# A state-space layer and a gated FFT convolution in one kernel: another order of its 815 operations

## The chip, the cores and the metric

The kernel runs on one core of one Trainium2 chip. The metric is the device time of one execution in microseconds. Three timed runs of the kernel before gave 187.6, 186.19 and 186.77 us; the median, 186.77, is the time that the change is held against.

## The reference

Two sequence layers on inputs of 2048 steps by 640 channels, written side by side into one output of 1280 channels:

```python
# A: a diagonal complex state-space layer
Lam_bar = exp(exp(log_dt) * (Lambda_re + 1j * Lambda_im))
B_bar = ((Lam_bar - 1) / Lambda)[:, None] * (B_re + 1j * B_im)
Bu = einsum("bld,pd->blp", x, B_bar)
h[t] = Lam_bar * h[t - 1] + Bu[t]                  # t = 0 .. 2047
y_A = 2 * einsum("blp,dp->bld", h, C).real + x * Dskip
# B: a short convolution, a gate, a long convolution, a gate
k_shift[t] = sum(k[t - 3 + i] * shift_k[:, 3 - i] for i in range(4)) # four taps
kv = k_shift * v
y = irfft(rfft(kv, 4096) * rfft(ssm_k, 4096))[:2048]
y_B = q * (y + kv * ssm_D)
out = concatenate([y_A, y_B], axis=-1)
```

All inputs and the output are bfloat16.

## The kernel before, in words

The program is built in two steps. First `build` calls methods of `PartA` and `PartB`, which record 815 operations with `Program.add`: a name, the engines that may do it, what it reads and writes in one large SBUF array (`arena`), and its PSUM group. Nothing is issued by that. Then `Program.emit` goes through the table `ORDER` (L1117) from left to right and issues each operation on the engine that stands in the table. An entry such as `561A4` is operation 561, on ScalarE (A; V is VectorE, G GpSimd, T TensorE, S the DMA queue of SyncE), with its PSUM group from bank 4 on. A small `t` is TensorE too, and puts the operation in `P.narrow`: its matmuls are then issued as two halves of 64 columns of weights each (`wide`, L225 for a whole one, L229 for a half; s1 has the same at L876 and L881). There are 8 banks, and most groups take two, so up to four groups are in flight. Each engine does its entries in the order of the table; waits between engines follow from what the operations read and write and from who held the bank last. So the table sets the order on each engine, the engine of each operation that has a choice, the banks, and the halves. Nothing else of the kernel decides an order.

Part A, the state-space layer, scans by a tree. The complex state is kept as pairs of real rows, ten groups of 128.

- up2, up1, up0: projections of x (`base`, L581) and additions of shifted terms by tables of powers (RR, made at L457 on VectorE; its matmuls are L602). ScalarE or VectorE copies the result out of PSUM (ev_up, L598, L622, L648).
- the coarse scan, in two halves 0 and 1: a swap by matmul (cs_v, cs_k, by `wide`), its product with a sine (cs_v_m, cs_k_m, L679), cs_a L682, cs_w L683, the scan cs_s L684, cs_b L687 and cs_h L690, all on VectorE.
- dn and ad: the way down, a matmul and an addition (L728 on VectorE; on ScalarE the sum is made by TensorE and L726 copies it).
- gC and ev_gC: C scaled by matmul (L571) and copied (L575).
- C0 to C15: 128 rows of the output each. ld_r loads rows of x (L736), xd multiplies them by Dskip (L737, on VectorE or GpSimd; Dskip is loaded by ld_Dr, L372), 20 matmuls make C (L225, or 40 halves at L229), and ev_C adds (L754 on VectorE; or a copy on ScalarE, L752, and the addition em_C on GpSimd, L760). L765 stores.

Part B, the gated convolution.

- per 128 channels: k and v come transposed (L814), the taps cm (L205 on VectorE, L206 on ScalarE), additions ca L840, the gate cx L841, and a copy to DRAM (pl, L847). The relay rl loads that back in another layout, eight pieces for each half of the channels (L857, sixteen in all).
- s1 and s2: the two stages of the forward transform, of the filter ("h", loaded at L807, with addD L809) and of kv ("k"), for each half (s1k0, s1k1 and so on), by matmuls (L876 or L881, then L900), with copies e1 (L886) and e2 (L913).
- the product of the two spectra, four pieces for each half: pp L924, pq L927, py L929, pz L931.
- r2 and r1: the two stages of the inverse transform (L951, L972). r2 of one half reads all four py and pz of that half. er2 copies (L956). er1 multiplies by q: on VectorE directly (L990), on ScalarE as a copy (L988) with the product em1 after it on VectorE or GpSimd (L995). q is loaded at L825, and L1006 stores.

The names carry the half and the first index: er10_22 is the eviction of r1 of half 0, block 22; cm3_2 is tap 2 of channel group 3. The table interleaves both parts on every engine.

Of the kernel before, what the change touches and what calls it, by code (L numbers as in the profile page):

```python
# [1097 lines left out]
def plain_order(P):  # L1098
# [19 lines left out]
    "168A0 156G0 161S0 0V0 58G0 6T0 17G0 167A0 162S0 110G0 19V0 147G0 87V0 11G0 18V0 89A0 90S0 12G0 3T1 42G0 13V0 88S0 182S0 "  # L1118
    "67G0 22V0 4T0 25V0 171T1 26G0 23V0 65V0 148G0 39V0 66V0 112G0 59V0 72G0 9T0 183S0 165T2 46G0 30G0 169T0 69G0 180S0 92T3 "
    "5T4 93V3 20V0 10T5 111G0 94A0 68G0 166A2 95V0 1T4 163T5 32V0 160G0 2T4 181S0 124V0 122V0 102V0 164A5 31V0 127V0 96V0 8T2 "  # L1120
    "103V0 21V0 104V0 61V0 172A1 7T4 126V0 105V0 28V0 14V0 106V0 219T2 60V0 101A0 107V0 100A0 36V0 98A0 108V0 170A0 123V0 37V0 "
    "173S0 38V0 128V0 33V0 109V0 40V0 62V0 114G0 317V0 113G0 125V0 27V0 115G0 29V0 41V0 116G0 117G0 149G0 221T0 220A2 174S0 "
    "118G0 43G0 97A0 99A0 119A0 44G0 211T2 222V0 155S0 63A0 151G0 378S0 71A0 15A0 47G0 70A0 209T0 212V2 152G0 45A0 120V0 50G0 "
    "121V0 178S0 213T2 131V0 210A0 52G0 143V0 159A0 74G0 187S0 179S0 217T0 381A0 146V0 51G0 34A0 227T4 380A0 129V0 186S0 48G0 "
    "130V0 185S0 214A2 382V0 77G0 215T6 218A0 54G0 132V0 228V4 157S0 73G0 383A0 237T0 133V0 35V0 82G0 134V0 184S0 216A6 83G0 "
    "384V0 49A0 379S0 55G0 261T6 385A0 56G0 78G0 253T4 53A0 386V0 79G0 75A0 389S0 262V6 238A0 225T2 150G0 254A4 188V0 176S0 "
    "57A0 84G0 387V0 201T4 154A0 177S0 195T6 245T0 196A6 202V4 390S0 226A2 391V0 392V0 191T2 246A0 136V0 229T4 393V0 269S0 "
    "192A2 394V0 76A0 395V0 153A0 223T2 396V0 230A4 144V0 400S0 141A0 203T0 224A2 189T4 135V0 145V0 239T6 81A0 388S0 64V0 397V0 "
    "204A0 401S0 140A0 190A4 398V0 199T0 193t2 16A0 138A0 231T4 403V0 194A2 137V0 24V0 402V0 271S0 142A0 200A0 404V0 80A0 197T0 "
    "405V0 240A6 247T2 406V0 198A0 232A4 399S0 407V0 86A0 408V0 444S0 241T6 248A2 205T0 242A6 315V0 249T2 139A0 206A0 233T4 "  # L1130
    "250A2 409V0 243T6 411S0 207T0 234A4 244A6 251T2 235T4 255T6 252A2 175V0 410S0 208A0 415S0 236A4 85A0 320V0 316V0 158S0 "
    "447V0 301T4 256A6 313T0 446V0 302A4 318t2 257T6 319V2 314A0 309T4 448V0 258A6 311T2 414S0 310A4 259T6 299T0 416S0 321V0 "
    "413S0 260A6 449V0 303T4 312A2 263T6 412S0 322V0 304A4 272S0 300A0 450V0 305T0 264A6 451V0 323t4 417S0 297T2 306A0 324V4 "
    "418S0 265T6 445S0 298A2 273T0 266V6 281T4 325V0 267T6 274A0 285T2 282V4 268A6 307T0 286A2 326V0 327t4 295T6 329V0 308A0 "
    "275T2 328V4 296A6 293T0 276V2 423t4 724S0 294A0 330V0 455S0 279T6 336T2 331V0 280A6 431T0 424A4 334V0 332T6 337A2 277T4 "
    "333V6 432A0 287T2 270S0 278V4 433T6 288A2 335V0 425T0 729S0 452V0 434A6 338t4 440S0 419T2 441S0 426A0 339V4 421T6 453G0 "
    "420A2 422V6 429t0 340t4 442S0 430A0 435T2 341V4 342t6 346t7 436A2 427T0 343V6 289T4 347V7 428A0 437t2 290V4 350t6 438A2 "
    "458V0 439S0 344t4 457V0 351A6 283T0 501T2 345V4 459G0 284A0 348t6 502A2 91S0 466T0 349V6 352t4 467A0 291T2 353V4 470T6 "
    "292A2 477T0 471A6 490T2 478V0 734S0 468T4 491A2 456S0 499T6 460V0 479T0 469A4 726t2 461V0 500A6 443V0 480A0 725V0 602S0 "
    "462A0 524t0 727V2 532t6 522t4 730V0 731T2 728S0 525A0 454S0 463V0 739S0 533A6 472V0 464G0 523A4 503T6 732V2 366t0 504A6 "  # L1140
    "481T4 744S0 367V0 528T2 482A4 358t6 529A2 514T4 359V6 368t0 515A4 520T2 369V0 356t6 521A2 518T4 735G0 465S0 357V6 519A4 "
    "354T0 733S0 492T2 603S0 355V0 493A2 516t4 740G0 488T6 517A4 526t2 474V0 530t0 527A2 741t4 475V0 531A0 483V0 749S0 489A6 "
    "608S0 605S0 594T6 485G0 604S0 742V4 590T0 595A6 588T2 591V0 584T4 589A2 607S0 582T6 745V0 598T0 736t2 606S0 599A0 486V0 "
    "473V0 585A4 609S0 494V0 583A6 600T4 596T6 737V2 601A4 496G0 372t0 597A6 586T4 373V0 592T2 587A4 580T6 593V2 374t0 581A6 "
    "612T4 497G0 375V0 610t2 613A4 618T6 611A2 619V6 616T4 628T0 617A4 624T2 484V0 620t6 625A2 505V0 746T4 621A6 476V0 629A0 "
# [83 lines left out]
```

## Time and profile before

| what | value |
|---|---|
| timed runs | 187.6, 186.19, 186.77 us |
| the profiled execution: span from the first to the last instruction | 187.3 us |
| the profiled execution's own time | not given beside the span |
| mean granted TensorE clock | 0.999 of full speed |
| DMA | 30.15 MB, mean 161 GB/s |
| instruction fetches on q8 | 26 packets, 0.43 MB |

How to read the lines that follow. The page gives for each engine its busy time in us, its share of the span, and the number of instructions (PE is TensorE's matmuls, PEld its weight loads, DVE VectorE, ACT ScalarE, POOL GpSimd). A line of the waits names the waiting engine and line, what it waited for, and then the total in us, the times, and the longest. A line of the timeline has the start, the duration, the engine and the line, the operation with output and input, the number of instructions, and in brackets the idle time before it and what ended it; `issue` stands where the profile shows nothing that was waited for. SPq is SyncE's queue of DMA issues: there the duration is that of issuing. In the line groups, the number behind the count is busy us, then mean ns of one, then idle us before them. A line of the windows has the stretch, its length, then busy us and instructions of PE, PEld, DVE, ACT and POOL, and the granted clock, the DMA share and GB/s.

### The profile page before, as it was taken

What the parts mean: (1) busy time and instruction counts of PE and PEld (TensorE: products, weight loads), DVE (VectorE), ACT (ScalarE), POOL (GpSimd) and SP (SyncE); (2) the same over time, 40 slices, a digit from 0 to 9 for tenths busy, and PEclk for the clock granted to TensorE, in tenths of its full rate; (3) what the DMA queues carried; (4) which work ended last, traced back from release to release, by engine and by line L of the source; (5) the groups of instructions that cost most, each with busy time, mean ns of one, the idle gap of its engine ahead of it and who ended that gap; (6) DMA issues with size and microseconds to landing.
All of it is one profiled execution on the core that took longest, in us unless ns stands there. A gap on an engine that the chain in (4) does not pass through costs nothing.

```text
span 187.3 us, 7665 instructions
## 1 busy us (share of the span) xinstructions
PE 175.6 (94%) x3398; PEld 126.3 (67%) x3399; DVE 158.0 (84%) x225; ACT 147.7 (79%) x181; POOL 72.6 (39%) x68
## 2 busy tenths in 40 slices
PE   7998999999799979979997999999999999999992
PEld 2565666677468756656685688776588876887770
DVE  3537964679959899999969999899999999998961
ACT  2469699989899979999997997997898883985000
POOL 8679999900000000008803925730740000551620
PEclk9999999999999999999999999999999999999999
DMA  5999999799999989999989479402496993058996
GB/s 153 191 184 158 200 143 140 141 174 182 198 253 154 290 179 152 180 182 154 138 109 251 154 170 133 75 5 72 122 196 120 210 227 85 15 160 187 208 219 173
DMA packets 106682, 30.15 MB, mean 161 GB/s; under 512 B 101274, under 2 KB 106010, under 8 KB 106650
## 3 DMA queue, kind: packets, MB, share of 16 engines
q1 hardware_dynamic: 106332, 29.35, 86.7%
q8 instruction: 26, 0.43, 1.1%
q10 hardware_dynamic: 318, 0.33, 0.6%
q14 instruction: 6, 0.05, 0.1%
HBM read 11.32 MB, written 7.86 MB: 102 GB/s over the span
## 4 chain that ended last, share of the span: by engine, by line
PE 54%; DVE 23%; DMA 9%; ACT 8%; issue 3%; DVEq 0%; ACTq 0%
PE acc L225 17%; PE acc L581 13%; DMA arena<-in_B_k_dram 9%; PE acc L229 6%; DVE arena L728 6%; PE acc L900 6%; DVE arena L205 5%; ACT arena L913 5%; PE acc L951 4%; DVE arena L840 3%; PE acc L972 3%; PE acc L539 2%; DVE arena L754 2%; PE acc L881 1%; ACT arena L886 1%
## 5 line engine op out<-in xcount | busy, mean ns | idle before, releaser
L581 PE MATMUL acc<-arena 128*64 128x512 bf16 x400 | 45.6, 380 | 1.8 <-DVE arena L457 1.1
L913 ACT CAST arena<-acc 128x960 bf16<-128x960 f32 (+1 forms) x43 | 37.4, 916 | 4.0 <-PE acc L900 2.2
L225 PE MATMUL acc<-arena 128*128 128x320 bf16 (+2 forms) x255 | 36.4, 297 | 2.2 <-DVE arena L754 1.1
L581 PEld LDWEIGHTS <-arena 128*64 128x64 bf16 x400 | 26.0, 110 | 17.8 <-DVE arena L457 1.3
L886 ACT CAST arena<-acc 128x1024 bf16<-128x1024 f32 x37 | 35.8, 1034 | 2.1 <-PE acc L881 2.0
L225 PEld LDWEIGHTS <-arena 128*128 128x128 bf16 x256 | 23.7, 98 | 12.1 <-DVE arena L754 1.3
L841 POOL TENSOR_TENSOR arena<-arena 128x2048 bf16<-128x2048 bf16 x2 | 8.8, 4410 | 53.7 <-DVE arena L840 46.1
L900 PE MATMUL acc<-arena 128*64 128x160 bf16 x512 | 23.6, 235 | 1.8 <-DVE arena L679 1.4
L900 PEld LDWEIGHTS <-arena 128*64 128x64 bf16 x512 | 18.6, 110 | 8.3 <-ACT arena L913 2.2
L229 PE MATMUL acc<-arena 128*64 128x320 bf16 (+3 forms) x258 | 23.2, 313 | 0.5 <-DVE arena L690 0.5
L840 DVE TENSOR_TENSOR arena<-arena 128x2048 bf16<-128x2048 bf16 x14 | 17.6, 1256 | 4.5 <-ACT arena L206 4.3
L728 DVE TENSOR_TENSOR arena<-acc,arena 128x1024 bf16<-128x1024 f32 (+2 forms) x19 | 20.4, 1114 | 0.9 <-PE acc L229 0.5
L760 POOL TENSOR_TENSOR arena<-arena 128x640 bf16<-128x640 f32 x3 | 4.2, 1416 | 32.6 <-ACT arena L752 32.6
L956 ACT CAST arena<-acc 128x1024 bf16<-128x1024 f32 x16 | 15.4, 1025 | 1.7 <-PE acc L951 1.6
L229 PEld LDWEIGHTS <-arena 128*64 128x64 bf16 x258 | 13.0, 110 | 3.5 <-DVE arena L690 0.6
L876 PE MATMUL acc<-arena 128*64 128x128 bf16 x400 | 14.6, 220 | 0.2 <-ACT arena L886 0.2
L876 PEld LDWEIGHTS <-arena 128*64 128x64 bf16 x400 | 12.9, 110 | 2.4 <-ACT arena L886 0.9
L205 DVE TENSOR_SCALAR arena<-arena 128x2048 bf16<-128x2048 bf16 x15 | 11.0, 749 | 3.6 <-DMA arena<-in_B_k_dram 3.5
L754 DVE TENSOR_TENSOR arena<-acc,arena 128x640 bf16<-128x640 f32 x13 | 10.7, 820 | 3.5 <-PE acc L225 2.2
L206 ACT ACTIVATE arena<-arena 128x2048 bf16<-128x2048 bf16 (+2 forms) x10 | 11.1, 1112 | 1.5 <-DMA arena<-in_B_k_dram 1.5
L924 DVE TENSOR_TENSOR arena<-arena 128x2560 bf16<-128x2560 bf16 x8 | 11.9, 1484 | 0.1
L602 PE MATMUL acc<-arena 128*64 128x256 bf16 (+2 forms) x140 | 11.6, 291 | 0.1
(142 smaller groups left out, 284.4 us busy)
## 6 DMA issues: line engine op xcount, KB each, us to landing
out_dram<-arena SPq DMA_DIRECT2D x32, 160.0 KB, 3.3
arena<-in_B_ssm_k_dram SPq DMA_DIRECT2D x8, 320.0 KB, 6.1
kv_rows<-arena SPq DMA_DIRECT2D x5, 512.0 KB, 4.7
arena<-kv_rows SPq DMA_DIRECT2D x16, 160.0 KB, 4.0
arena<-in_A_x_dram SPq DMA_DIRECT2D x16, 160.0 KB, 3.5
arena<-in_B_q_dram SPq DMA_DIRECT2D x8, 320.0 KB, 6.3
arena<-in_A_B_im_dram ACTq DMA_DIRECT2D x1, 160.0 KB, 2.8
arena<-in_A_B_re_dram SPq DMA_DIRECT2D x1, 160.0 KB, 3.0
```

The lines of the kernel that those rows point to most:

```text
L205: vm = lambda e: lambda out, in_, by: e.tensor_scalar_mul(out=out, in0=in_, scalar1=by)
L225: e.matmul(out, lhsT=lhsT, rhs=rhs, start=start, stop=stop, skip_group_check=True)
L229: e.matmul(out[half], lhsT=lhsT[:, half], rhs=rhs, start=start, stop=stop, skip_group_check=True, tile_position=(0, 64 * r))
L581: e.matmul(o[64 * r:64 * r + 64], lhsT=self.BT[j][:, r, d, :], rhs=self.XP[:, d, 2 * q:2 * q + 2], start=(d == 0), stop=(d == 4), skip_gro ...
L728: e.tensor_tensor(out=o, in0=b, in1=o, op=ALU.add)
L754: e.tensor_tensor(out=two(ys), in0=two(B)[:, :, 0:320], in1=two(ys), op=ALU.add)
L840: P.add(f"ca{d}_{j}", tt, lambda e: e.tensor_tensor(out=t1, in0=t1, in1=t2, op=ALU.add), outs=[t1], ins=[t1, t2])
L876: e.matmul(B[64 * b:64 * b + 64, 128 * i:128 * i + 128], lhsT=lh[i], rhs=F[:, b, :], start=True, stop=True, tile_position=(0, 64 * b))
L886: P.add(f"e1{what}{hf}_{u}", {PACT: act(1024), PDVE: dve(1024)}, lambda e, B: c.CP[e](out=out, in_=(B.rearrange("p (l n s k) -> p k s l n" ...
L900: e.matmul(B[64 * s:64 * s + 64, 512 * b + 160 * i:512 * b + 160 * i + 160], lhsT=c.W[:, k, 64 * b:64 * b + 64], rhs=self.AS[hf][:, k, 160 ...
L913: c.CP[e](out=out, in_=b.rearrange("p r (k j n) -> p r k j n", k=n, j=4) if nj > 1 else b.rearrange("p r (k x) -> p r k x", k=n))
L956: P.add(f"er2{hf}_{u}", {PACT: act(1024), PDVE: dve(1024)}, lambda e, B: c.CP[e](out=out, in_=B.rearrange("p (s n b) -> p b s n", s=2, n=4 ...
```

## The change

Only `ORDER` changes: the table has the same 815 operations in another order, with other banks, and with other engines for some. TensorE's 214 operations come in nearly the same sequence, with local exchanges.

- No longer in halves: cs_v1, dn3_5, dn2_0, dn2_9, dn1_4, dn0_3, dn0_8, s1k0_5, s1h1_8, s1k1_0, s1k1_5, s1k1_6. Newly in halves: cs_k1, dn1_6, dn0_2, s1k0_3, s1k1_7, C5, C6, C9, C11. TensorE's matmuls and weight loads together go from 6798 to 6838.
- From ScalarE to VectorE: ev_up20_4, ev_up21_6, ev_up1_2, cm0_3, three small copies cf, js1, er10_6, er10_22, er10_12, er21_9, er11_0. From VectorE to ScalarE: ev_up20_2, e1h0_6, one cf, ev_gC2_0, er10_16, er21_8.
- From VectorE to GpSimd: xd1, xd8, xd11, xd15. From GpSimd to VectorE: the small memset k0 and em_C operations whose eviction is now on VectorE, which leaves them empty. em10_6, em10_12, em10_22 and em11_0 fall away, because VectorE multiplies directly; em10_16 appears.
- On SyncE the relay rl1_30 is the last of its eight, behind one load of q and the store of C3; ld_r15 stands behind the store of C8.

The diff replaces 43 lines of numbers by 41. One line of each:

```diff
-    "560T2 651V0 778S0 566T6 781T4 669V0 567A6 555A0 671V0 672V0 787T0 786V0 780V0 670V0 782A4 561A2 673V0 640V0 563T4 788A0 "
+    "539A0 669V0 554T4 786G0 776V6 560T2 555A4 563T0 561V2 777V0 778S0 573T6 676S0 781T4 768G0 574A6 564V0 562G0 670V0 565V0 671V0 "
```

Here 561 and 564 are er10_6 and er10_22, 786 is xd11, 768 is xd8, 669 is a pp1, 776 is ev_C9, and 640 and 673 are pz1.

Three places in the order of the engines. On VectorE, around the first half of the coarse scan. Before:

```order
L841 TENSOR_TENSOR arena<-arena 128x2048
L457 TENSOR_TENSOR arena<-arena 128x1280
L682 TENSOR_TENSOR arena<-arena 128x640
L668 MEMSET arena 128x10
L205 TENSOR_SCALAR arena<-arena 128x2048 x2
L679 TENSOR_TENSOR arena<-acc,arena 128x640
L840 TENSOR_TENSOR arena<-arena 128x2048
L683 TENSOR_TENSOR arena<-arena 128x640
```

With the change:

```order
L457 TENSOR_TENSOR arena<-arena 128x1280
L841 TENSOR_TENSOR arena<-arena 128x2048
L682 TENSOR_TENSOR arena<-arena 128x640
L679 TENSOR_TENSOR arena<-acc,arena 128x640
L683 TENSOR_TENSOR arena<-arena 128x640
L205 TENSOR_SCALAR arena<-arena 128x2048 x2
L668 MEMSET arena 128x10
L684 SCALAR_TENSOR_TENSOR arena<-arena 128x640
```

The steps cs_v0_m (L679) and cs_w0 (L683) moved ahead of the two taps of channel group 3 (L205, cm3_2 and cm3_3) and of an addition (L840). The L457 at the head of both pieces is the table for gC. Some thirty rows earlier on the same engine, the second of the tables RR (L457 too) moved up likewise: it now stands ahead of the gate cx0 (L841).

On SyncE, the queue of DMA issues around the load of Dskip (L372). Before:

```order
L814 DMA_TRANSPOSE arena<-in_B_v_dram 128x2048
L736 DMA arena<-in_A_x_dram 128x640
L814 DMA_TRANSPOSE arena<-in_B_k_dram 128x2048
L556 DMA_TRANSPOSE arena<-in_A_C_re_dram 128x1x640
L736 DMA arena<-in_A_x_dram 128x640
L807 DMA arena<-in_B_ssm_k_dram 32x80x64 x4
L372 DMA arena<-in_A_Dskip_dram 128x640
L736 DMA arena<-in_A_x_dram 128x640
L814 DMA_TRANSPOSE arena<-in_B_v_dram 128x2048
```

With the change:

```order
L556 DMA_TRANSPOSE arena<-in_A_C_re_dram 128x1x640
L814 DMA_TRANSPOSE arena<-in_B_v_dram 128x2048
L814 DMA_TRANSPOSE arena<-in_B_k_dram 128x2048
L807 DMA arena<-in_B_ssm_k_dram 32x80x64 x4
L372 DMA arena<-in_A_Dskip_dram 128x640
L736 DMA arena<-in_A_x_dram 128x640 x2
L814 DMA_TRANSPOSE arena<-in_B_v_dram 128x2048
```

The rows of x for C0 and C1 (the first two L736) moved from ahead of the four filter loads (L807, ld_h1) to behind them and behind Dskip; the rows for C2 moved behind v.

On VectorE, the end of the products of half 1. Before:

```order
L924 TENSOR_TENSOR arena<-arena 128x2560
L927 TENSOR_TENSOR arena<-arena 128x8x160
L929 TENSOR_TENSOR arena<-arena 128x8x4x40
L737 TENSOR_TENSOR arena<-arena 128x640 x2
L927 TENSOR_TENSOR arena<-arena 128x8x160
L931 TENSOR_TENSOR arena<-arena 128x8x4x40 x2
L990 TENSOR_TENSOR arena<-acc,arena 128x2x12x40
```

With the change:

```order
L924 TENSOR_TENSOR arena<-arena 128x2560
L754 TENSOR_TENSOR arena<-acc,arena 128x640
L990 TENSOR_TENSOR arena<-acc,arena 128x2x12x40 x2
L927 TENSOR_TENSOR arena<-arena 128x8x160 x2
L931 TENSOR_TENSOR arena<-arena 128x8x4x40
L929 TENSOR_TENSOR arena<-arena 128x8x4x40
L737 TENSOR_TENSOR arena<-arena 128x640
L931 TENSOR_TENSOR arena<-arena 128x8x4x40 x2
L990 TENSOR_TENSOR arena<-acc,arena 128x2x8x40
```

Two evictions with product (L990, er10_6 and er10_22) now stand ahead of the last pq1, py1 and pz1 (L927, L929, L931), where ScalarE did them before (L988); one L737 less stands there, since xd11 is on GpSimd.

76 rows, old and new, of the table ORDER are left out of this document.

## The prediction

> **What bounds the kernel now.** I read the busy line and the slices first, then the waits, then stretches.
>
> ```profile
> PE 175.6 (94%) x3398; PEld 126.3 (67%) x3399; DVE 158.0 (84%) x225; ACT 147.7 (79%) x181; POOL 72.6 (39%) x68
> ```
>
> TensorE is busy for 94% of the span; 187.3 - 175.6 = 11.7 us is all that it idles. An order can only win from that, or lose to it.
>
> ```profile
> PE acc L900 <- DVE arena L679: 1.4, 1, 1.4
> PE acc L581 <- DVE arena L457: 1.1, 1, 1.1
> DVE arena L737 <- DMA arena<-in_A_Dskip_dram: 1.4, 1, 1.4
> ```
>
> The longest waits of TensorE (total, times, longest) are for VectorE. The windows (us, then busy of PE, PEld, DVE, ACT, POOL) tell who sets the pace:
>
> ```profile
> 9.20:41.10 31.90, 31.27 (x323) 20.49 (x325) 21.02 (x39) 27.92 (x35) 27.03 (x28) 1.00 1.14 162
> ...
> 54.00:82.80 28.80, 25.95 (x509) 18.90 (x504) 27.70 (x38) 26.95 (x41) 0.00 (x0) 1.00 1.07 204
> ...
> 97.90:138.20 40.30, 38.57 (x908) 28.51 (x895) 38.58 (x41) 35.90 (x42) 20.62 (x9) 1.00 0.59 128
> 138.20:161.50 23.30, 23.08 (x570) 18.34 (x568) 22.77 (x29) 18.00 (x22) 0.00 (x0) 1.00 0.83 147
> 161.50:170.10 8.60, 8.60 (x221) 7.41 (x212) 8.10 (x12) 6.73 (x7) 4.79 (x3) 1.00 0.39 114
> 170.10:187.30 17.20, 13.50 (x336) 9.92 (x324) 10.95 (x12) 1.92 (x2) 5.00 (x3) 0.99 0.86 204
> ```
>
> Up to 41 us TensorE has 31.27 of 31.90 while VectorE is a third idle: what the table exchanges there (three evictions of the up-sweep come from ScalarE to VectorE, two go back) can win 0.6 at most, and I count it 0. From 54 us on VectorE is as full as TensorE; from 97.9 on it idles 1.72 + 0.53 = 2.25 us in 63.6. The hinge is the end of the products:
>
> ```profile
> 159.82 1.68 DVE L931 TENSOR_TENSOR arena<-arena 128x1280 bf16<-128x1280 bf16 x2
> 161.65 1.54 PE L951 MATMUL acc<-arena 64*128 64x128 bf16 x43
> ```
>
> The last product sum (pz1, L931) ends at 161.50 and the first inverse transform (r21, L951) starts at 161.65; it reads all four pz1. So I follow VectorE to that point, and TensorE from it: 25.65 us to the end.
>
> **Part 1, coarse scan, -1.6.** The second of the tables RR (L457) and the two steps cs_v0_m (L679) and cs_w0 (L683) move up on VectorE, the latter past the two taps (L205) that wait for k.
>
> ```profile
> 47.98 0.16 DVE L440 TENSOR_TENSOR arena<-arena 128x10 f32<-128x10 f32 x1
> 65.20 1.42 DVE L205 TENSOR_SCALAR arena<-arena 128x2048 bf16<-128x2048 bf16 x2 [0.65 <-DMA arena<-in_B_k_dram]
> 66.53 0.82 DVE L679 TENSOR_TENSOR arena<-acc,arena 128x640 bf16<-128x640 f32 x1
> L575 DVE CAST arena<-acc 128x640 bf16<-128x640 f32 x4 | 3.3, 815 | 0.0
> ```
>
> Both waits of TensorE (1.4 + 1.1 = 2.5 us) can go, which is the best bound: TensorE's idle moves to nothing else in that stretch. But VectorE has to run its whole list before the second scan ends (cs_h1, 82.8). It idles 28.80 - 27.70 = 1.10 there, 0.65 of it for k, which the moved steps now fill. One C eviction (L575, 0.82) leaves for ScalarE; three small copies (cf) come over from it and one goes there, 0.16 each as the nearest row of 10 columns. 1.10 + 0.82 - 0.32 = 1.6, of bounds 0 (k comes late at the taps as before, and the list waits there) and 2.5. ScalarE, busy 26.95 of 28.80, has the 0.8 us for that eviction.
>
> **Part 2, the x rows behind ld_h1, +1.1.** Two loads of x rows (L736) go from ahead of the filter loads (L807) to behind them and behind Dskip (L372).
>
> ```profile
> 77.68 0.53 SPq L736 DMA_DIRECT2D arena<-in_A_x_dram  x1
> 81.83 0.53 SPq L736 DMA_DIRECT2D arena<-in_A_x_dram  x1
> 82.93 7.61 SPq L807 DMA_DIRECT2D arena<-in_B_ssm_k_dram  x4
> 90.58 3.45 SPq L372 DMA_DIRECT2D arena<-in_A_Dskip_dram  x1
> 97.87 0.49 DVE L737 TENSOR_TENSOR arena<-arena 128x640 bf16<-128x640 bf16 x1 [1.38 <-DMA arena<-in_A_Dskip_dram]
> arena<-in_A_x_dram SPq DMA_DIRECT2D x16, 160.0 KB, 3.5
> 99.37 2.89 PE L225 MATMUL acc<-arena 128*128 128x320 bf16 x20 [0.97 <-DVE arena L754]
> ```
>
> The product xd0 (L737) waited for Dskip, issued until 94.03. In the changed order Dskip's issue starts up to 1.1 earlier (two issues of 0.53), so ends near 93.0; the row load behind it takes 0.5 to issue and lands 3.5 after: 97.0 to 97.5. So xd0 starts 0.4 to 0.8 earlier, not 1.6: I take 0.5, and 1.1 of part 1 is lost in the queue. Bounds: nothing gained, or the whole 1.6 if the row lands in time. Behind xd0 on VectorE stand the eviction of C0 and every product to come, and TensorE waits for that eviction (the 0.97 at 99.37, where C1 wants its bank). Of the two loads the later one moves past the four filter quarters and Dskip, the earlier one past k and a part of C too; these are all issued up to a microsecond earlier; v, the next behind them, is issued at much the same time as before.
>
> **Part 3, VectorE's list from xd0 to the last pz1, +1.3.** Two evictions with product (er10, L990) come over from ScalarE and now stand ahead of that pz1; two xd (xd1, xd11) leave for GpSimd.
>
> ```profile
> L990 DVE TENSOR_TENSOR arena<-acc,arena 128x960 bf16<-128x960 f32 x3 | 3.5, 1150 | 0.3 <-PE acc L972 0.3
> L995 DVE TENSOR_TENSOR arena<-arena 128x960 bf16<-128x960 bf16 x3 | 2.0, 652 | 0.7 <-ACT arena L988 0.7
> L737 DVE TENSOR_TENSOR arena<-arena x11: 481/484/1685, 97.9 to 175.0; 128x640 bf16<-128x640 bf16 x11
> L737 POOL TENSOR_TENSOR arena<-arena x5: 1396/1397/1647, 106.1 to 179.6; 128x640 bf16<-128x640 bf16 x5
> 159.12 0.69 ACT L752 COPY arena<-acc 128x640 f32<-128x640 f32 x1 [2.62 <-issue]
> 159.71 0.96 ACT L988 CAST arena<-acc 128x960 bf16<-128x960 f32 x1
> ```
>
> 2 x 1.15 - 2 x 0.48 (481 ns, the shortest L737) = +1.34 on a list with almost no idle. ScalarE did these evictions for nothing: it had just idled 2.62. I let 0.3 fall into VectorE's own idle (2.25 in the stretch) and add 0.3 for GpSimd (below): +1.3. Bounds: -0.9, if all idle could be filled, to +4.1 with both GpSimd products fully in the way (2 x 1.40).
>
> So r21 starts at 161.65 - 0.5 + 1.3 = 162.45.
>
> **Part 4, the tail, -0.2.** After pz1 VectorE's list is lighter: the two er10 bring no L995 behind them (2 x 0.65). ScalarE and VectorE empty r21's banks between them, and VectorE is busy 8.10 of 8.60. But TensorE runs that window without a gap, so the gain is limited to matmuls that stretch for a bank; 0.2 of bounds 0 and 0.6.
>
> The last stretch (17.20 with 13.50 of TensorE) has the same C steps and the same stores in another order. xd15 goes to GpSimd (1.40 for 0.48), its row load behind one more store: the eviction of C15 may come 0 to 0.9 later, and I take 0, since C12 wants that bank only after C14 (a C step lasts 2.9) and a part of r11.
>
> **Part 5, instruction blocks, 0.** The table changes which TensorE steps are split in halves: twelve no longer are and nine newly are, +40 TensorE instructions. On TensorE that costs nothing, since a C step in 40 halves lasted as long as one in 20 whole matmuls (2.88 below, and the 2.89 of C1 above); so only the fetches matter.
>
> ```profile
> q8 instruction: 26, 0.43, 1.1%
> 84.60 0.17 PEld L881 LDWEIGHTS <-arena 64*64 64x64 bf16 x9 [0.18 <-issue]
> 158.07 0.93 PEld L225 LDWEIGHTS <-arena 128*128 128x128 bf16 x8 [0.41 <-issue]
> 94.59 2.88 PE L229 MATMUL acc<-arena 128*64 128x320 bf16 x40
> ```
>
> 26 fetches came, and two waits of the weight loads without a releaser fall on a border between them, 0.18 and 0.41 us. Moving the borders is worth 0.6 at best; all other blocks were there in time. The larger of the two lies at 158, where pz1 sets the next start anyway, 3.6 us later. So 0, and if a border of the changed order falls badly, the loss is of the same size, 0.6. The Trainium skill ("Runtime: NRT & Kernel Launch", Instruction fetch mechanics) says that blocks of 256 instructions are fetched ahead and that a boundary is mostly hidden; by that rule the sum would be the same, 0 against at most -0.6 by the rows.
>
> **Sum.** -1.6 + 1.1 + 1.3 - 0.2 + 0 = +0.6 on a profiled span of 187.3. The page gives no time of its own for that execution; the span lies within the three timed runs (186.19 to 187.6), 0.5 above their median. I put the difference on the median: 186.77 + 0.6 = 187.4 us.
>
> **The rivals.** (a) TensorE's removed waits carry through. For it: TensorE is fuller than VectorE over the whole span, VectorE's idle of 2.25 could take the 1.34, and the end of the products could move with TensorE. Against: pz1 ends just as r21 starts. It gives 186.77 - 1.6 - 0.2 = 185.0, and with the whole 2.5 and 0.2, 184.1.
>
> (b) GpSimd's products hold VectorE: slower. The trace has it on L737, of which part 3 shows the shortest (481 ns) and the longest (1685 ns, the one at 175.0):
>
> ```profile
> 112.31 2.62 POOL L927 TENSOR_TENSOR arena<-arena 128x1280 bf16<-128x1280 bf16 x1 [3.42 <-DVE arena L924]
> 112.53 0.82 DVE L754 TENSOR_TENSOR arena<-acc,arena 128x640 bf16<-128x640 f32 x1 [0.37 <-PE acc L229]
> 114.44 0.83 DVE L737 TENSOR_TENSOR arena<-arena 128x640 bf16<-128x640 bf16 x1
> 174.72 1.65 POOL L737 TENSOR_TENSOR arena<-arena 128x640 bf16<-128x640 bf16 x1
> ```
>
> The one at 114.44 lasted until 0.34 after GpSimd's L927 had ended (114.93), and beside GpSimd's own L737 one took 1.69. The L754 at 112.53, which reads PSUM, took its usual 0.82 beside the same L927. The change brings four more L737 (xd1, xd8, xd11, xd15) to GpSimd, 1.40 each; in the table xd11 and xd8 stand beside L754 and the two L990, PSUM readers too, so they may cost nothing. It decides from the point where xd11's row lands 1.5 us earlier or later than the place in the list: then both fall among products from SBUF, 2.8 in place of the 0.3 that I took, 187.4 + 2.5 = 189.9. The Trainium skill ("SBUF — State Buffer", SBUF: two separate sides) calls this an exclusive lock, held for a whole instruction, against a VectorE operation with two SBUF inputs; the trace agrees, with 0.83 and 1.69 for 0.48.
>
> (c) A relay is late: slower.
>
> ```profile
> 110.08 7.08 SPq L857 DMA_DIRECT2D arena<-kv_rows  x6
> 121.75 0.45 PE L881 MATMUL acc<-arena 64*64 64x64 bf16 x32
> arena<-kv_rows SPq DMA_DIRECT2D x16, 160.0 KB, 4.0
> ```
>
> The relay rl1_30, which s1k1_0 (L881) reads, was among these six, and is now issued last, behind a load of q and a store. The six ended at 117.16; one issue more (7.08 / 6 = 1.2) is 118.4, and with 4.0 to land 122.4. TensorE wants it at 121.75 - 0.5 = 121.25: 1.2 late, and as much again where the store ahead waits for its rows. This decides from the point where the landing passes 121.25; 187.4 + 1.8, between the two, is 189.2. Against it: as long as SP runs ahead by the 0.5 to 1.1 of the earlier start, the row may just be there.
>
> (d) Everything lies beside the path: 186.8.
>
> **How the numbers follow.** A measurement here tells about 1% (1.9 us) from no change. Forecast 0.44 (of it 0.02 over 188.6), (a) 0.24 (0.17 under 184.9, as the whole 2.5 is what the rows allow), (b) 0.14 (0.13 slower), (c) 0.06 (slower), (d) 0.12. Faster 0.17, slower 0.21, same 0.62. The likeliest case alone has 186.4 to 188.6. The range: down to 184.6, which leaves out the lower half of (a), 0.1; up to 189.3, which leaves out (b)'s full price, 0.1.
>
> **What would show it.** Right: no wait of L900 on L679 and of L581 on L457; xd0 gated by an x row near 97.3; two L990 before the last L931, which ends near 162.3, with r21 right behind; 25.4 us from there. Wrong: r21 more than 1 us ahead of 161.65, or L931 ending well before r21 starts (then TensorE sets the pace, (a)); L737 or L93x on VectorE over 1.2 (b); a wait of L881 or L876 for kv_rows (c).

## The result and the profile after

| | median of the runs | range | ratio to before |
|---|---|---|---|
| before | 186.87 us | 186.19 to 187.6 (5 runs) | |
| the changed kernel | 200.73 us | 199.5 to 203.25 (5 runs) | 1.071 [1.066, 1.076] |

The change makes the kernel 7% slower: +13.9 us by the medians and +13.3 by the ratio, where +0.6 was predicted, and 11 us above the range. The profiled execution of the changed kernel has a span of 200.8 us and took 202.56, which is 1.8 above its median: 1.8 us lie outside the span, as in its other runs (200.73 had a span of 199.0). So the 187.3 of before's profile stands for some 189.1 (an estimate, with the same 1.8), which is 2.2 above before's median; that its span lies "within the three timed runs", as the prediction has it, says nothing of its time. Some executions of a kernel fall into a slower state, and every ratio here leaves these out (of exp_er a single run is left, so it has none), while medians and ranges count all runs.

The busy line and the granted clock in the 40 slices, after:

```profile
PE 181.0 (90%) x3419; PEld 124.2 (62%) x3419; DVE 162.0 (81%) x226; ACT 147.5 (73%) x178; POOL 78.3 (39%) x71
...
PEclk9999996999999999999996999999999999999997
```

TensorE is busy 181.0 us for the work that took 175.6, and idles 19.8 instead of 11.7. Two slices, from 30 and from 105 us, have a clock of 6 tenths. Its waits (for what, then total, times, longest):

```profile
PE acc L581 <- ACT arena L598: 3.0, 1, 3.0
PE acc L225 <- DVE arena L754: 2.2, 1, 2.2
PE acc L524 <- DMA arena<-in_A_B_re_dram: 1.4, 1, 1.4
...
PE acc L972 <- DVE arena L754: 1.1, 1, 1.1
PE acc L225 <- DVE arena L990: 0.9, 1, 0.9
```

The two waits that the change was to remove (L900 for L679, L581 for L457) are gone. In their place stands a longer one, for a ScalarE eviction of the up-sweep (L598), in the stretch that the prediction counted as 0. Where the time goes is seen by following single steps of TensorE through both traces. After:

```profile
30.52 4.04 PE L581 MATMUL acc<-arena 128*64 128x512 bf16 x20 [3.04 <-ACT arena L598]
...
34.82 2.32 PE L581 MATMUL acc<-arena 128*64 128x512 bf16 x20
...
106.12 4.41 PE L225 MATMUL acc<-arena 128*128 128x320 bf16 x20 [2.19 <-DVE arena L754]
...
173.00 5.44 PE L951 MATMUL acc<-arena 64*128 64x128 bf16 x160
...
181.19 1.77 PE L972 MATMUL acc<-arena 64*64 64x80 bf16 x176
...
189.53 0.91 PE L972 MATMUL acc<-arena 64*64 64x80 bf16 x80
```

And before, those that were not shown yet:

```profile
169.91 1.77 PE L972 MATMUL acc<-arena 64*64 64x80 bf16 x176
...
177.15 0.91 PE L972 MATMUL acc<-arena 64*64 64x80 bf16 x80
```

C1 starts 6.75 us later (106.12 against 99.37) and takes 1.52 longer; r21 starts 11.35 later (173.00 against 161.65), the first r11 11.28, the last r11 12.38, and the span ends 13.5 later. In these two traces more than half (6.75 + 1.52 = 8.3) is lost by the end of C1.

### The profile page after: what moved, and what is told of

It reads as the page before. It is cut to its first block, busy times and chain, and to the rows that moved or that the text cites. A ratio compares the mean times of both kernels' runs of the same rounds, so it can differ in the third digit from the quotient of the medians.

```text
span 200.8 us, 7717 instructions
## 1 busy us (share of the span) xinstructions
PE 181.0 (90%) x3419; PEld 124.2 (62%) x3419; DVE 162.0 (81%) x226; ACT 147.5 (73%) x178; POOL 78.3 (39%) x71
## 4 chain that ended last, share of the span: by engine, by line
PE 55%; DVE 16%; ACT 12%; DMA 6%; SPq 6%; issue 3%; DVEq 0%
PE acc L581 19%; PE acc L229 9%; PE acc L225 9%; DVE arena L728 6%; PE acc L602 4%; SPq L807 4%; PE acc L900 4%; PE acc L951 4%; PE acc L876 3%; DMA arena<-in_A_x_dram 2%; DMA arena<-in_A_B_re_dram 2%; PE acc L972 2%; DVE arena L754 2%; DMA arena<-in_A_B_im_dram 2%; DVE arena L927 2%
## 5 line engine op out<-in xcount | busy, mean ns | idle before, releaser
L581 PE MATMUL acc<-arena 128*64 128x512 bf16 x400 | 47.1, 390 | 3.7 <-ACT arena L598 3.0
L581 PEld LDWEIGHTS <-arena 128*64 128x64 bf16 x400 | 22.6, 113 | 24.6 <-ACT arena L598 3.5
L229 PE MATMUL acc<-arena 128*64 128x320 bf16 (+3 forms) x394 | 33.0, 310 | 0.8 <-ACT arena L886 0.5
L225 PE MATMUL acc<-arena 128*128 128x320 bf16 (+3 forms) x188 | 29.0, 306 | 4.0 <-DVE arena L754 2.2
L841 POOL TENSOR_TENSOR arena<-arena 128x2048 bf16<-128x2048 bf16 x2 | 8.1, 4068 | 54.4 <-ACT arena L886 51.9
L225 PEld LDWEIGHTS <-arena 128*128 128x128 bf16 x188 | 17.5, 101 | 12.5 <-DVE arena L754 2.3
L229 PEld LDWEIGHTS <-arena 128*64 128x64 bf16 x394 | 20.8, 110 | 6.3 <-ACT arena L886 0.8
L900 PE MATMUL acc<-arena 128*64 128x160 bf16 x512 | 23.4, 235 | 0.9 <-DVE arena L728 0.5
L737 POOL TENSOR_TENSOR arena<-arena 128x640 bf16<-128x640 bf16 x9 | 13.0, 1452 | 26.8 <-DMA arena<-in_A_x_dram 26.8
L900 PEld LDWEIGHTS <-arena 128*64 128x64 bf16 x512 | 18.9, 110 | 6.5 <-DVE arena L728 1.7
L840 DVE TENSOR_TENSOR arena<-arena 128x2048 bf16<-128x2048 bf16 x14 | 18.7, 1339 | 1.2 <-ACT arena L206 0.9
L754 DVE TENSOR_TENSOR arena<-acc,arena 128x640 bf16<-128x640 f32 x13 | 10.7, 821 | 9.8 <-PE acc L225 4.2
L876 PE MATMUL acc<-arena 128*64 128x128 bf16 x448 | 16.2, 221 | 0.5
L876 PEld LDWEIGHTS <-arena 128*64 128x64 bf16 x448 | 13.7, 110 | 3.9 <-ACT arena L886 1.0
L205 DVE TENSOR_SCALAR arena<-arena 128x2048 bf16<-128x2048 bf16 (+1 forms) x18 | 12.9, 730 | 0.2
L924 DVE TENSOR_TENSOR arena<-arena 128x2560 bf16<-128x2560 bf16 x8 | 12.3, 1532 | 0.2
L927 DVE TENSOR_TENSOR arena<-arena 128x1280 bf16<-128x1280 bf16 x14 | 11.2, 818 | 0.1
```

What stands on the lines that cost most here:

```text
L225: e.matmul(out, lhsT=lhsT, rhs=rhs, start=start, stop=stop, skip_group_check=True)
L229: e.matmul(out[half], lhsT=lhsT[:, half], rhs=rhs, start=start, stop=stop, skip_group_check=True, tile_position=(0, 64 * r))
L581: e.matmul(o[64 * r:64 * r + 64], lhsT=self.BT[j][:, r, d, :], rhs=self.XP[:, d, 2 * q:2 * q + 2], start=(d == 0), stop=(d == 4), skip_gro ...
L840: P.add(f"ca{d}_{j}", tt, lambda e: e.tensor_tensor(out=t1, in0=t1, in1=t2, op=ALU.add), outs=[t1], ins=[t1, t2])
L876: e.matmul(B[64 * b:64 * b + 64, 128 * i:128 * i + 128], lhsT=lh[i], rhs=F[:, b, :], start=True, stop=True, tile_position=(0, 64 * b))
L900: e.matmul(B[64 * s:64 * s + 64, 512 * b + 160 * i:512 * b + 160 * i + 160], lhsT=c.W[:, k, 64 * b:64 * b + 64], rhs=self.AS[hf][:, k, 160 ...
```

## The table loads: what the prediction did not read

ScalarE's timeline of the changed kernel, from 18 us:

```profile
18.68 1.28 ACT L388 ACT_TABLE_LOAD   x1
19.97 0.21 ACT L388 ACTIVATE arena<-arena 128x10 f32<-128x10 f32 x1
20.19 1.28 ACT L414 ACT_TABLE_LOAD   x1
21.48 0.27 ACT L414 ACTIVATE arena<-arena 128x80 f32<-128x80 int32 x1
21.75 1.28 ACT L388 ACT_TABLE_LOAD   x1
23.05 0.21 ACT L388 ACTIVATE arena<-arena 128x10 f32<-128x10 f32 x1
23.17 0.99 ACT L598 CAST arena<-acc 128x1024 bf16<-128x1024 f32 x1
24.18 1.28 ACT L314 ACT_TABLE_LOAD   x1
...
29.48 1.90 ACT L598 CAST arena<-acc 128x1024 bf16<-128x1024 f32 x2
```

L388 is an exponential, L414 and L314 are sines. In these rows each change from the one to the other brings a row ACT_TABLE_LOAD of 1.28 us, in which ScalarE loads the table of the other function, and the new order puts two of the five exponentials of L388 alone between sines. Four loads stand in these 6 us, ahead of two up-sweep evictions whose banks TensorE wants: its wait of 3.04 ends when the first of these evictions is done. The line groups show all loads, in before

```profile
L383 ACT ACT_TABLE_LOAD x1 | 1.3, 1283 | 2.3 <-DVE arena L258 2.3
L414 ACT ACT_TABLE_LOAD x1 | 1.3, 1283 | 0.0
```

and after:

```profile
L388 ACT ACT_TABLE_LOAD x2 | 2.6, 1283 | 0.0
...
L206 ACT ACT_TABLE_LOAD x1 | 1.3, 1283 | 2.1 <-DVE arena L247 2.1
L289 ACT ACT_TABLE_LOAD x1 | 1.3, 1283 | 0.0
L414 ACT ACT_TABLE_LOAD x1 | 1.3, 1283 | 0.0
L314 ACT ACT_TABLE_LOAD x1 | 1.3, 1283 | 0.0
```

Two loads have become six: 4 x 1.283 = 5.1 us of ScalarE. The Trainium skill ("ScalarE: Activation LUTs", Table sets: the hidden batching unit) says that functions of different sets cost a load at every switch. The trace agrees on that. The page's figure of about 2.7 us for a load, which counts a drain with it, does not fit: a load takes 1.283 here, and the next operation starts right behind it (18.68 + 1.28, then 19.97).

**The theory** was then: the loads cost 4 to 6 us of the loss, and the rest lies in the x rows (part 2) and VectorE's list (part 3). **Rivals:** the instruction blocks; or the whole loss lies in the last third, and the loads are hidden.

## The experiments

In the diffs a token is an operation's number, its engine (T TensorE, t TensorE in halves, A ScalarE, V VectorE, G GpSimd, S SyncE) and its bank. Only `ORDER` is edited; the computation is the same in all.

**exp_together**, the changed kernel with its exponentials in one group (97 to 101 are those of L388):

```diff
-114G0 101A0 ... 63A0 48G0 100A0 119A0 155S0 97A0 120V0
+114G0 101A0 100A0 97A0 ... 63A0 48G0 119A0 155S0 120V0
```

> The changed kernel with two small exponentials (rn, L388) moved up on ScalarE to stand behind the other three, nothing else. Two table loads are left of six, 5.1 us less of ScalarE before 25 us. Theory (table loads): TensorE's wait of 3.0 for L598 and its slow matmuls behind it go, 194.5 to 197.5 us. Rival (ScalarE had the time, and the late second load of B and the rest make the loss): 199 us or more.

194.87 us (193.39 to 197.56), 1.0394 [1.0337, 1.0451]: 5.9 us less than the changed kernel's 200.73, and within what was expected. TensorE no longer waits for L598, and the same up-sweep matmuls run through:

```profile
21.73 8.58 PE L581 MATMUL acc<-arena 128*64 128x512 bf16 x78
```

**before_six_tables**, the other way round: before with two exponentials moved apart (119 and 71 are sines), which makes six loads:

```diff
-118G0 43G0 97A0 99A0 119A0 44G0 ... 378S0 71A0 15A0
+118G0 43G0 119A0 97A0 44G0 ... 378S0 71A0 99A0 15A0
```

> The kernel before with two of its five small exponentials (rn, L388) moved down on ScalarE, one behind al_s (L414) and one behind the next sine (L354): six table loads for two, nothing else. Theory (table loads): 5.1 us more of ScalarE in a stretch where it was busy 27.92 of 31.90, its evictions of the up-sweep come late and TensorE waits: 190 to 192.5 us. Rival (the loads alone are absorbed, and only the changed order made them hurt): 187 to 188.5 us.

192.79 us (191.99 to 193.24), 1.0294 [1.0224, 1.0364]: +5.5 on the 187.26 of before measured beside it, a little above what was expected. The wait of the changed kernel appears in before's order:

```profile
24.41 10.51 PE L581 MATMUL acc<-arena 128*64 128x512 bf16 x80 [3.18 <-ACT arena L598]
```

80 such matmuls at exp_together's 8.58 / 78 are 8.8 us; here they take 1.7 more, behind a wait of 3.18. Both directions together show it: the four loads are worth 5.5 to 5.9 us. That is a little more than their 5.1; TensorE also runs slowly after the wait, which fits, but was not tested apart.

**front_before and front_after**, splices at the first xd: before's order up to there and the changed one behind it, and the reverse. They were to say which side of 97 us the loss lies on.

> The table of before up to the first product with Dskip (xd0, L737), then the changed table for all that is left. Theory (table loads): ScalarE loads its activation tables six times in the changed order and twice before, at 1.28 us each, and the slow start makes most of the loss; without it the rest costs what the late x rows and the longer list of products cost by the two traces, 12.4 - 4.9 = 7.5 us at most: 190 to 194.5 us. Rival (all is early): the later loss only follows from the disturbed start: 186 to 188 us.

> The changed table up to xd0, then the table of before. Theory (table loads, then separate late losses): the 4.9 us that C0 started late stay, 190.5 to 193 us. Rival (all is early, and grows by itself): 197 us or more.

front_before 195.49 us (194.04 to 200.19), 1.0414 [1.0348, 1.048]; front_after 196.79 us (194.99 to 199.37), 1.0491 [1.0406, 1.0575]. Neither fits its theory or its rival. The sum, 8.2 + 9.5, is more than 13.9, so a splice adds a loss of its own. In front_before TensorE has waits that neither parent has: 2.2 us at L876, 1.5 at L225 and 1.4 at L972, all without a releaser, 5.1 us in all. A splice has another number of TensorE instructions ahead of each step, so the borders of the instruction blocks lie elsewhere. This made the blocks a suspect, and the splices no clean measure.

**x_rows_ahead**, undoing part 2 alone in the changed kernel (724 and 729 are the two x rows):

```diff
-424A4 332t6 455S0 ... 434A6 439S0 ... 491A0 724S0 ... 460V0 729S0 468T2
+424A4 332t6 724S0 455S0 ... 434A6 729S0 439S0 ... 491A0 ... 460V0 468T2
```

> The changed kernel with the loads of x rows for C0 and C1 (L736) ahead of the four filter loads again. Theory: C1 and what follows no longer wait for the eviction of C0 and the product on GpSimd, of the 3.5 us lost between C1 and s2k0_30 two to three come back: 197.5 to 198.8 us. Rival (the slow start has made everything late and these rows are not what is missing): 200 us or more.

201.16 us (199.06 to 202.11), 1.0719 [1.0643, 1.0795]: nothing gained, as the rival had it. **exp_rows** does the same on exp_together, and also moves ld_r9 (773) up to stand behind 767:

> The changed kernel with the exponentials together (as in the run before) and with the loads of x rows earlier on SyncE: those for C0 and C1 ahead of the filter loads, that for C9 ahead of two loads of q. Theory (late x rows): the two idle times of VectorE before L737, 1.67 and 1.68 us in the run with the exponentials together, go: 191 to 193 us, of 194.9. Rival (the rows were late beside the path, and the products held by GpSimd and the added evictions set r21's start): 194 us or more.

197.34 us (196.81 to 198.3), 1.0543 [1.0482, 1.0605], worse than exp_together. In x_rows_ahead TensorE's wait at C1 falls from 2.19 to 0.81, but the filter loads, now behind the rows, come late for the step before it (0.6 us of such a wait in the changed kernel):

```profile
102.54 1.04 PE L881 MATMUL acc<-arena 64*64 64x64 bf16 x96 [1.54 <-DVE arena L809]
```

In exp_rows the addition L809 waits 2.1 us for that load (`in_B_ssm_k_dram`). This fits a queue of SyncE that is late as a whole at this place, where another order only passes the wait on.

**exp_er** (er10_6 and er10_22, 561 and 564, back on ScalarE in exp_together, their products em behind er21) and **exp_rows_er** (exp_rows and that):

```diff
-563T0 561V2 777V0 ... 574A6 564V0 562G0 670V0 565V0 671V0
+563T0 561A2 777V0 ... 574A6 564A0 670V0 671V0 ... 687V4 565V0 562V0
```

> The changed kernel with the exponentials together and with er10_6 and er10_22 back on ScalarE (L988), their products (L995) on VectorE behind the evictions of r21, as before. Theory (VectorE's list up to the last pz1): r21 starts 2 us earlier, 192 to 193.5 us, of 194.9. Rival (late rows): 194.5 us or more.

> All three edits: exponentials together, x rows earlier, er10_6 and er10_22 on ScalarE. If the table loads, the late rows and the longer list are the whole loss: 187 to 190 us. If something else in the order of the second half is missing (GpSimd's products beside VectorE's, the relay behind q): 191 us or more.

exp_er 196.98 us (193.44 to 199.35), inconclusive; exp_rows_er 196.82 us (195.29 to 198.09), 1.0507 [1.0419, 1.0594], no gain over exp_rows, and far from the 187 to 190 that all three edits were to give. In exp_together r10 waits for VectorE, and so does C1:

```profile
100.82 2.89 PE L225 MATMUL acc<-arena 128*128 128x320 bf16 x20 [1.82 <-DVE arena L754]
...
159.43 0.48 PE L972 MATMUL acc<-arena 64*64 64x80 bf16 x32 [1.63 <-DVE arena L754]
```

With VectorE's list shortened, exp_rows_er has a wait without a releaser a step later instead:

```profile
160.27 2.20 PE L225 MATMUL acc<-arena 128*128 128x320 bf16 x15 [2.14 <-issue]
```

**before_blocks**, before with C5 and C6 in halves, +80 instructions on TensorE and nothing else; it moves the borders of the blocks so that one holds almost only r10, another only r11:

```diff
-507V0 751T4 748S0 ... 649V0 757T4 543A2
+507V0 751t4 748S0 ... 649V0 757t4 543A2
```

> The kernel before, in its own order, with two more TensorE steps in halves (C5 and C6): +80 instructions, which cost TensorE nothing by themselves. From there on each border of 256 instructions falls 80 earlier in the work, so that one block is made of r10 alone and one of r11 alone (L972, 192 instructions in about 1.05 us). Theory (blocks): two waits without a releaser of 2 to 3.3 us, as in the run with the changed end, 189.5 to 193 us. Rival (blocks are hidden, part 5 of the prediction): 186.5 to 187.6 us.

193.42 us (191.8 to 195.02), 1.027 [1.0186, 1.0353]: +5.1 by the ratio for splitting forty matmuls, clear of no change, though not clearly above 2%. TensorE:

```profile
150.19 1.48 PE L972 MATMUL acc<-arena 64*64 64x80 bf16 x142
155.15 0.54 PE L972 MATMUL acc<-arena 64*64 64x80 bf16 x18 [3.48 <-issue]
155.62 6.77 PE L225 MATMUL acc<-arena 128*128 128x320 bf16 x40
...
175.62 5.47 PE L225 MATMUL acc<-arena 128*128 128x320 bf16 x39 [2.02 <-issue]
```

r10's 142 matmuls, with a weight load each 284 instructions, are gone in 1.48 us; then TensorE stands 3.48 us in the middle of the same step, and the profile shows nothing that it waits for. The traces show no fetch itself; that the blocks are the cause rests on these waits coming, as expected here, and going (cut_blocks, below) with the number of instructions ahead alone. The Trainium skill ("Runtime: NRT & Kernel Launch", Instruction fetch mechanics) calls the crossing of a block "mostly hidden". The trace disagrees in this run, with 3.48 and 2.02 us.

**before_halves** takes the changed kernel's set of halves into before's order (+40 instructions, 21 tokens such as `332T6` to `332t6`).

> The kernel before with the changed kernel's choice of TensorE steps in halves, in the order of before: +40 TensorE instructions, and the borders of the instruction blocks lie elsewhere. Theory (blocks are hidden, part 5): 187 to 187.6 us. Rival (a block that falls badly costs one to two us, as the waits of 1 to 2.2 us without a releaser in three of the runs above suggest): 188.3 us or more.

187.81 us (186.49 to 190.1; 10 runs), 1.0027 [0.9995, 1.0058]: the halves by themselves cost nothing. Its waits at TensorE begin with

```profile
PE acc L225 <- DVE arena L754: 1.2, 1, 1.2
PE acc L539 <- DVE arena L535: 1.0, 1, 1.0
```

and it has neither the 1.4 for L679 nor the 1.1 for L457, though its order there is before's. Nor have the other six traces with before's order up to there (before_blocks, front_before and the four cut runs below): at most 0.4 for L679, and none for L457.

**before_scan_first**, part 1 alone in before (319 and 321 are cs_v0_m and cs_w0, 447 and 446 the two taps, 144 the second RR):

```diff
-57A0 84G0 387V0 ... 230A4 144V0 ... 158S0 447V0 301T4 256A6 313T0 446V0 ... 319V2 314A0 ... 416S0 321V0
+57A0 84G0 144V0 387V0 ... 230A4 ... 158S0 301T4 256A6 313T0 ... 319V2 321V0 447V0 446V0 314A0 ... 416S0
```

> The kernel before with part 1 of the prediction alone: the second table RR (L457) ahead of cx0, cs_v0_m (L679) and cs_w0 (L683) ahead of the two taps that wait for k; SyncE's queue as before. If the early gain is real and carried by VectorE's idle in front of xd0: 185.5 to 186.5 us. If Dskip's landing, which sets xd0, takes it all back: 187 us, no change.

188.03 us (187.09 to 188.89; 10 runs), 1.0052 [1.0018, 1.0085]: half a per cent slower, where part 1 had -1.6. VectorE now stands 1.02 us at the moved step L679, waiting for TensorE's L229.

**cut_products and cut_blocks**, before up to pp1 of half 1 (some 138 us), and the changed order from there; cut_blocks has C6, C7, C9 and C11 whole as well, to move the borders:

```diff
-763t2 ... 757t2 ... 775t6 ... 787t0
+763T2 ... 757T2 ... 775T6 ... 787T0
```

**cut_products_er and cut_blocks_er** are the same two with er10_6 and er10_22 on ScalarE and xd11 and xd8 (786, 768) on VectorE behind them, which undoes part 3.

> The table of before up to the first product of half 1 (pp1, near 138 us), then the changed table. Theory (part 3 of the prediction is right in size, 1.3 us, and the tail changes little): 188 to 189.5 us. Rival (the changed end holds more of the loss than its own list, by GpSimd's products or TensorE's instruction blocks): 190.5 us or more.

> As the run above, with er10_6 and er10_22 on ScalarE, xd11 and xd8 on VectorE at their places of before. Theory (VectorE's list sets r21's start): 1 to 2 us less than the run above, 187 to 188 us. Rival: the same as the run above.

> The run with the table of before up to the first product of half 1 and the changed table behind it, with C6, C7, C9 and C11 whole: the borders fall 120 to 160 instructions later, each block there holds a C step. Theory (blocks): the waits of 2.06 and 3.21 us go, 190 to 192.5 us, of 196.6. Rival (the changed end is slow by its lists): 195 us or more.

> The same with er10_6 and er10_22 on ScalarE, xd11 and xd8 on VectorE. Part 3 of the prediction (VectorE's list sets r21's start, +1.3): 1 to 2 us less than the run above, and within 1.5 us of before. Rival (without the blocks' waits VectorE's list has no slack to lose): the same as the run above.

| | median us (range) | ratio |
|---|---|---|
| cut_products | 196.6 (195.26 to 199.73) | 1.0475 [1.0413, 1.0538] |
| cut_products_er | 194.85 (193.27 to 196.4) | 1.0378 [1.0307, 1.0449] |
| cut_blocks | 190.25 (190.22 to 191.3) | 1.0143 [1.0085, 1.0202] |
| cut_blocks_er | 190.04 (189.78 to 191.2) | 1.013 [1.0069, 1.0192] |

cut_products has two of the waits at blocks:

```profile
155.91 0.51 PE L972 MATMUL acc<-arena 64*64 64x80 bf16 x34 [2.06 <-issue]
...
175.97 0.55 PE L972 MATMUL acc<-arena 64*64 64x80 bf16 x19 [3.21 <-issue]
```

Four C steps made whole take them away, and some 6 us with them (1.0475 to 1.0143). What is left, 190.25 against the 187.65 of before measured beside it, +2.6, is the new order of the last third itself. There VectorE's list sets r21, as part 3 said; in cut_blocks

```profile
163.24 4.93 PE L951 MATMUL acc<-arena 64*128 64x128 bf16 x144 [1.15 <-DVE arena L931]
```

and in cut_blocks_er:

```profile
160.86 5.42 PE L951 MATMUL acc<-arena 64*128 64x128 bf16 x160
```

r21 starts 2.4 us earlier, without a wait, but the median is only 0.2 lower, where 1 to 2 were expected. Of the 2.4, 0.9 was there before the edit (the first L951 starts at 142.33 and 141.45), so the edit is worth 1.5 at r21. Behind r21, cut_blocks_er gives 1.1 of this back: ahead of the last two C steps TensorE waits 1.12 us for an eviction (L754), which had itself waited 3.27 for an xd on GpSimd, whose row of x came late. In cut_blocks it does not wait there. VectorE's list is longer by more than the two evictions alone:

```profile
156.83 2.80 DVE L927 TENSOR_TENSOR arena<-arena 128x1280 bf16<-128x1280 bf16 x2
```

These two products stand in cut_blocks beside the two xd on GpSimd (155.46 to 158.21); in cut_blocks_er, with these xd on VectorE, they take 1.55. That is the mechanism of the prediction's rival (b), at 1.25 us.

**exp_blocks and exp_blocks_row_er**, exp_together with C6 and C9 whole (`757t2` to `757T2`, `775t6` to `775T6`), the latter with ld_r9 earlier and the er10 on ScalarE as well; **exp_b**, exp_together with the loads of B and of the parameters on the queues and in the order of before.

> The changed kernel with the exponentials together and C6 and C9 whole, so that no block of 256 instructions there holds r10 alone. If the block's wait comes beside VectorE's (r10_28 waited 1.63 us for the eviction of C9 in the run with the exponentials together, and the block arrives behind it): 194 to 195.5 us, no change. If the blocks add to it: 191.5 to 193.5 us.

> The same, with the x rows of C9 loaded earlier and er10_6 and er10_22 on ScalarE, which takes VectorE's wait away too. With both waits gone r21 starts 3 to 4 us earlier than with the exponentials together alone: 190.5 to 192.5 us. What is left to the time of before is then the later start and the x rows of C0, some 3 us. If it stays above 194 us, something else sets the second half.

> The changed kernel with the exponentials together and, besides, the four loads of B and the three of parameters on the queues and at the place that they have before (one load of B was issued at 4.87 by ScalarE, behind its first operation, and TensorE waited 1.35 us for it). Theory: the first up-sweep starts 2 us earlier, 192 to 193.5 us, of 194.9. Rival (VectorE and ScalarE take it back before C0): 194.5 us or more.

195.34 us, 1.0436 [1.0377, 1.0494]; 195.12 us, 1.0402 [1.032, 1.0484]; 195.81 us, 1.0426 [1.0335, 1.0516]. None differs from exp_together's 194.87. For exp_blocks that was one of the two expectations: the wait at a block lies behind VectorE's there, so taking it away alone frees nothing. exp_blocks_row_er was expected at 190.5 to 192.5 us, with both waits gone. From C1 to r21 its trace is 2.0 us shorter than that of exp_together (63.75 against 65.77), but C1 starts 1.0 later, behind a wait for B of 2.9 us in place of 2.2, and TensorE waits 0.98 us for an eviction ahead of the last two C steps. exp_b replaces TensorE's wait for B by one of 1.66 us for a parameter (`in_A_log_dt_dram`).

No version tried is faster than before.

## Why the prediction was wrong, point by point

- **The start, counted 0: this step failed.** "What the table exchanges there [...] can win 0.6 at most, and I count it 0" bounds a gain by TensorE's idle and takes that for the bound of a loss. A stretch that is full can lose any amount. ScalarE's own list was not read there: it was busy 27.92 of 31.90 before, the changed table has exponentials between the sines, and before's profile has the duration of a load, 1283 ns. 5.1 us of load on an engine with 4.0 idle could have been a term; it was put at nothing. Measured: 5.5 to 5.9.
- **Part 1, -1.6: wrong.** Alone it gives +1.0 (1.0052 of 187). The waits of 1.4 and 1.1 were read from one execution that was some 2.2 us longer than the median; seven other traces of the same order there have at most 0.4 of the first and none of the second. The step fails where a single profile's waits are taken for the kernel's.
- **Part 2, +1.1: the mechanism holds, the size does not.** xd0 waits for an x row, as predicted, though at 104.61 since all is late:

```profile
104.61 0.49 DVE L737 TENSOR_TENSOR arena<-arena 128x640 bf16<-128x640 bf16 x1 [1.78 <-DMA arena<-in_A_x_dram]
```

  C1 waits 2.19 for the eviction behind it (0.97 before) and then runs 1.52 slower: 2.7, not 1.1. But the 1.52 is this execution's alone, since C1 takes 2.89 in every other trace here. That undoing the move gains nothing (x_rows_ahead) fits a limit in the queue as a whole, not in the place in it.
- **Part 3, +1.3: the mechanism is right.** VectorE after, on the way to the last pz1:

```profile
165.53 2.21 DVE L990 TENSOR_TENSOR arena<-acc,arena 128x960 bf16<-128x960 f32 x2
...
171.00 1.68 DVE L931 TENSOR_TENSOR arena<-arena 128x1280 bf16<-128x1280 bf16 x2
```

  The second L931 ends at 172.68 and r21 starts at 173.00. By cut_blocks and cut_blocks_er the step costs 1.5 at r21, close to the 1.3, but 0.2 at the end. That it comes so close is partly luck: in cut_blocks 1.25 of VectorE's longer list is rival (b)'s, and in cut_blocks_er the list ends 1.85 us ahead of r21 (159.01 and 160.86), so there TensorE sets it.
- **Part 4, -0.2:** from r21 to the first r11 the lag goes from 11.35 to 11.28, nothing lost, within the bounds of 0 and 0.6. xd15 on GpSimd makes its eviction wait 3.0, not 0 to 0.9 (the waits have `DVE arena L754 <- POOL arena L737: 3.0, 1, 3.0`). That it costs nothing held in the changed kernel, where the next C step starts right behind r11; in cut_blocks_er it cost 1.12. Two losses were not in the sum: 0.93 at C14, which waits for an L990 on VectorE, and 1.1 between the last eviction and the end.
- **Part 5, 0 with 0.6 either way: right here, and wrong as a bound.** The changed kernel shows 0.26 us of such a wait. But the bound came from the borders that before happens to have. A moved border costs 2.0 to 3.5 us (before_blocks), and in the changed kernel one is hidden only because VectorE is late first (2.14 in exp_rows_er).
- **The rivals.** (b) hardly shows in the changed kernel: xd8 and xd11 stand beside L754 and the two L990 there, as the prediction had it, and the two L927 behind them take their usual 1.55; beside xd1 one L924 takes 1.85 for 1.48. In cut_blocks it does show, with 1.25. (c), the relay, does not show among TensorE's waits. None of the four had ScalarE in it.

**The account.** Of the +13.3 to 13.9, 5.5 to 5.9 is the table loads, shown from both sides. If the parts add up, 2.6 is the order of the last third (cut_blocks); that leaves about 5 before 138 us. The traces put about half of this at the very start. The first up-sweep matmul (L581) starts at 8.87 to 9.37 in ten traces with before's start. In nine with the changed start it starts at 9.59 to 13.34, the middle one at 11.82, and seven of these have a wait of TensorE for a load of B of 0.8 to 3.5 us ahead of it. This is read from single executions, and the one edit that aimed at it (exp_b) only put a wait for another load there (L581 at 11.56). So the remainder stays open: the late loads at the start, C1's wait, and VectorE's list are all to be seen, but each repair only passed the wait to the next load or engine, and no experiment took it away.

## What to carry to other kernels

Before costing a reordering, compare the full list of each engine, also where the trace says "full" or "hidden", and look for instructions that the order itself creates, such as table loads: a stretch without idle bounds the gain, never the loss. Take a wait as recoverable only when more than one execution has it, and set a profile's span plus what lies around it against the timed runs first. When a splice or a split shows a new wait with no releaser, count the instructions to the next border before blaming the order.

## What the runs showed of the hardware

- **A block of short matmuls can run out.** Where r10 or r11 were expected to fill a block (two instructions per matmul, 284 in 1.48 us), TensorE stood 2.06, 3.21, 3.48 us with no releaser. With C steps in the blocks (20 matmuls in 2.89 us) such a wait was at most 0.7 in before_halves.
- **A wait of 2 to 3 us can be paid twice, but its length alone does not decide.** Behind waits of 3.04, 2.19 and 3.48 us the next matmuls ran slowly: twenty of L581 4.04 for 2.32, C1 4.41 for 2.89, two C steps 6.77 for 5.61. Behind 1.82, 2.02 and 2.14 they did not (2.89 for 20, 5.47 for 39, 2.20 for 15). But one and the same trace, cut_products_er, has it the other way round:

```profile
156.13 0.77 PE L972 MATMUL acc<-arena 64*64 64x80 bf16 x34 [2.05 <-issue]
156.83 4.24 PE L225 MATMUL acc<-arena 128*128 128x320 bf16 x20
...
177.71 0.37 PE L972 MATMUL acc<-arena 64*64 64x80 bf16 x19 [2.94 <-issue]
178.01 5.61 PE L225 MATMUL acc<-arena 128*128 128x320 bf16 x40
```

  Slow behind 2.05, at full speed behind 2.94. Windows over the first two slow stretches in the changed kernel (stretch, length, then TensorE's busy us, the granted clock, DMA share, GB/s):

```profile
30.00:34.50 4.50, 3.98 (x22) 0.62 1.52 122
106.00:110.60 4.60, 4.48 (x24) 0.65 0.83 238
```

  The granted clock is 0.62 and 0.65 there. The Trainium skill ("TensorE: Matmul & The Clock Gate", What's actually happening) puts the drop behind an idle window of about 3.4 us; here slow matmuls were seen behind a wait of 2.05, and what decides between the two cases no run shows.
- **A table load takes 1.283 us** each time, whichever function asks for it, in each of the eight loads of the two kernels (two before, six after).
